# Two attention batches that sum keys and values in one pass each, with an instruction list arranged for it

## The chip, the cores and the metric

The kernel runs on one core of a Trainium2 chip. The metric is the device time of one execution in microseconds (us); lower is better. The core has a matrix engine (TensorE, in the profile PE, its weight loads PEld), VectorE (DVE), ScalarE (ACT), GpSimd (POOL) and SyncE (SP), each with its own queue of instructions that it works through in order. Engines wait for each other and for transfers through semaphores.

## The reference

Two stages. The first is an attention over 8 batches of 8 heads, 576 rows, 64 dimensions, in which keys and values are first pooled into 32 memory slots by a softmax of phi. The second is a bilinear feed-forward layer over all 4608 rows.

```python
a = exp(phi - max)                       # (8, 8, 576, 32)
a = a / (sum over the 32 slots)
k_m = einsum('bhsm,bhsd->bhmd', a, k)    # pooled keys, (8, 8, 32, 64)
v_m = einsum('bhsm,bhsd->bhmd', a, v)    # pooled values
scores = q @ k_m.T / sqrt(64)
attn = softmax(scores) @ v_m             # (8, 8, 576, 64)
x = attn, heads side by side             # (4608, 512)
out = ((x @ w_a) * (x @ w_b)) @ w_out    # w_a, w_b: (512, 1536), w_out: (1536, 512)
```

## The kernel before

Every instruction is issued from one list, the string `PLAN`, written out by hand or by a planner; the loop at the end of the kernel reads it token by token. So the order of tokens is the order of instructions on each engine. A wait in one instruction holds everything behind it on the same engine.

Tokens that begin with a digit are steps of that batch's attention:

- `exp0`, `exp1`: ScalarE takes the exponential of half of phi (L260).
- `qt0` to `qt3`: VectorE turns a quarter of q in 32 by 32 blocks (L269).
- `ks0`, `ks1` and `vs0`, `vs1` (`sums`): TensorE pools keys with a column of ones (L345, 128 columns), or values (64 columns), for one group of four heads, 36 matmuls each; VectorE then scales (L354, L355). `kt`, `vt` (`transpose`): small transposes into `kvT`, 8 for keys and 4 for values of a group (L363), and a copy (L366). These four serve batches 0 and 1 only.
- `kv` (`kv_sums`): keys, values and ones in one pass of 192 columns, 72 matmuls for all heads (L286). `km` (`take_kv`): VectorE scales into `rep` (L313, L318). `kvt` (`kv_transpose`): six full transposes and one copy (L326, L327). Batches 2 and later use `kv`.
- `s0`, `s1`: scores of a group (L380). `e0`, `e1`: ScalarE's exponential of them (L393). `den`: denominators by a matmul with `ones` (L403) and ScalarE's logarithm (L404). `nr`: ScalarE's exponential R (L412) and the product A on VectorE (L414). With a second digit, these take half of the rows.
- `hv`, `v` and `hx`, `x`: the fold of pooled values into 256 or 512 columns of w_a (a) or w_b (b) on TensorE (L449), and the copies of its result `vab` by ScalarE and VectorE (L462). The up projection then needs only A and `vab`.

The others: `aB.i.h` and `bB.i.h` are one half of an up projection of batch B, two matmuls (L624), then ScalarE's copy (L628) or VectorE's product into `ht` (L631). `dN` is N matmuls of the down projection (L553); `g`, `h`, `T` and `V` are its sums and differences on VectorE or POOL (L537, L520). `fN` and `FN` are N fill matmuls of 128 or 512 columns on a tile `warm`, whose results nobody reads (L211). `O` builds `ones` for the denominators, first on VectorE (L236), then on POOL (L237, L239). `M` is POOL's memset of the column of ones for batch 1's buffer (L642).

`pB`, `kB`, `vB`, `qB` load phi, k, v, q of a batch, `wLO:HI` a slice of columns of w_a and w_b, `oN` a part of w_out. All these are issued from POOL (L138 to L164). Phi keeps its four-byte type; k, v, q and weights become two-byte numbers on the way. `.0` or `.1` behind q is one half. Ahead of the list the kernel loads k of batch 0 in four-byte numbers on SP and ScalarE (L171; VectorE makes the cast, L217), then phi, q and v of batch 0 on POOL.

Of the kernel before, what the change touches and what calls it, by code (L numbers as in the profile page):

```python
# [35 lines left out]
a0.11.1 k2 d1 2exp0 g0.0 b1.6.1 b1.6.0 a1.9.1 h0.3 b0.11.1 v2 a0.10.1 b1.9.0 q2 T00 b0.10.1 T01 d1 a1.8.1 T21 d3
g0.1 V10 g0.2 d2 V20 a1.11.1 d1 2exp1 d1 V11 d3 b1.9.1 a1.10.0 a1.11.0 d3 b1.11.1 2kv 2km p3 b1.8.1 d1 q3 d4 k3
d2 a1.10.1 d9 a1.8.0 T31 d1 2kvt d1 2qt0 d2 2qt1 T30 3exp0 h1.0 d5 2qt2 d1 2qt3 d11 h1.1 b1.10.0 d1 3exp1
b1.11.0 d1 2sc g1.2 2e0 b1.8.0 g1.3 g2.0 v3 d1 2e1 d5 3qt0 d3 2den0 d1 2nr0 g2.1 d7 2v0 d1 3qt2 d1 p4 2den1 d5
2nr1 d7 p5 2x0b b1.10.1 2x0a d9 2v1 d3 a2.3.0 g2.2 a2.2.0 d2 3qt3 3qt1 2x1a d3 2x1b d1 a2.1.0 a2.0.0 h2.3 d3  # L40
# [1 line left out]
b2.0.0 p6 d1 b2.5.0 d7 b2.4.0 d1 3kvt a2.8.1 a2.7.0 d1 b2.8.0 d1 a2.6.0 b2.8.1 a2.11.1 d2 3sc 3e0 4qt0 d1 g3.1
d1 a2.7.1 d1 b2.7.0 d3 3e1 5exp0 d5 g3.2 b2.7.1 a2.11.0 4qt1 b2.6.0 b2.11.1 3den0 a2.4.1 d1 a2.5.1 b2.5.1 4qt2
d1 h3.3 d1 3nr0 a2.10.1 d1 b2.4.1 d3 b2.11.0 a2.0.1 d1 a2.9.0 d1 b2.10.1 4qt3 b2.9.0 d1 3den1 d1 a2.10.0 d1
b2.10.0 b2.0.1 d2 3v1 3x1a 4kv 3x1b 3v0b h4.0 3x0b a2.9.1 3nr1 d1 h4.1 h4.2 h4.3 a2.6.1 a2.3.1 a2.2.1 4km0 d1
4km1 4kvd b2.6.1 d2 5exp1 d13 b2.9.1 d2 3v2 3v0a 3x2b 3x2a d6 3x0a b2.2.1 d5 p7 a3.9.0 a3.11.0 b2.3.1 d3 5qt0
a3.1.0 b3.9.0 b3.1.0 b3.11.0 a3.3.0 d1 a3.0.0 b3.3.0 b3.0.0 v5 d4 a3.5.0 d4 a3.10.0 d2 b3.5.0 d2 4sc a2.1.1 d2
a3.10.1 d5 4e1 a3.4.1 d1 6exp0 b2.1.1 b3.10.0 4e0 4ed d1 b3.4.1 5qt3 g5.0 d3 a3.7.0 a3.8.1 b3.10.1 d1 a3.2.1
b3.8.1 b3.7.0 b3.2.1 a3.6.0 h5.1 d1 h5.3 b3.6.0 a3.1.1 q6 5qt1 a3.8.0 b3.1.1 h5.2 a3.3.1 a3.4.0 k6 a3.2.0 b3.2.0
b3.8.0 b3.3.1 d1 a3.6.1 4sm0 4v0a 5kv d1 5km0 d4 a3.9.1 d1 b3.4.0 4x0a d2 5km1 d1 h6.0 d4 a3.5.1 a3.7.1 v6 4tn0  # L50
d4 b3.6.1 b3.9.1 d2 h6.1 d4 a3.11.1 d1 4v1 4v0b d5 4x1b d1 a3.0.1 4x0b d1 4sm1 4x1a 5qt2 d1 6qt0 d1 b3.7.1 h6.2
4tn1 4ad 5kvd d9 4v2 d3 g6.3 d9 b3.11.1 d5 4x2a d10 b3.0.1 d1 6qt3 4x2b 7exp0 b3.5.1 6exp1 d3 h7.0 d9 a4.4.0
a4.0.0 a4.1.0 a4.5.0 b4.4.0 5sc 5e0 b4.0.0 a4.9.0 d1 5e1 b4.5.0 h7.1 b4.1.0 a4.11.0 b4.9.0 5v0 5x0a 6kv d1
a4.4.1 d1 h7.3 d1 6km0 d1 6km1 d1 5x0b 5ed d6 h7.2 d2 b4.4.1 a4.2.0 b4.11.0 a4.10.1 b4.10.1 b4.2.0 d1 h8.0
a4.6.1 d1 6kvd d1 5sm0 a4.1.1 a4.8.1 a4.7.0 5v1 6qt1 h8.1 q7 d1 5x1b b4.7.0 b4.6.1 k7 d2 b4.1.1 d3 5x1a d1
a4.2.1 a4.10.0 6qt2 b4.8.1 a4.6.0 5v2 5x2a 7exp1 d5 v7 b4.2.1 b4.6.0 d1 a4.8.0 d1 b4.10.0 a4.7.1 5x2b h8.3 d2
5tn0 d2 7qt0 b4.7.1 g8.2 d2 b4.8.0 a4.3.0 d7 5sm1 b4.3.0 d7 g9.0 d4 a4.9.1 d5 a4.3.1 d2 h9.1 d1 a4.5.1 d5 6sc d4
5tn1 6e1 d1 5ad b4.9.1 d1 a4.11.1 g9.2 d2 a4.0.1 d1 b4.5.1 b4.3.1 d3 6e0 d1 b4.0.1 g9.3 d1 b4.11.1 d4 6v0a 6v0b
6x0a 7kv d8 a5.2.0 7km0 d2 7km1 d2 7kvd d6 b5.2.0 6ed a5.2.1 6x0b b5.2.1 a5.11.0 d2 a5.9.0 a5.0.1 d4 b5.9.0 d8
7qt2 d1 h10.0 7qt1 d2 a5.3.1 g10.1 d8 b5.11.0 d1 b5.0.1 d2 h10.3 d1 a5.8.0 6sm0 a5.10.0 b5.3.1 b5.8.0 d4 a5.6.0  # L60
a5.1.1 b5.10.0 h10.2 7qt3 d1 a5.11.1 d3 a5.1.0 d1 b5.6.0 6tn0 d3 b5.1.1 a5.7.0 a5.0.0 b5.1.0 b5.11.1 a5.4.0
b5.0.0 b5.7.0 d2 a5.7.1 a5.4.1 b5.4.0 b5.7.1 d2 a5.3.0 6sm1 a5.10.1 6tn1 6v1 d1 6ad d1 6x1b b5.3.0 b5.4.1 d1
6x1a d1 b5.10.1 d3 6v2 d6 6x2b d1 6x2a a5.5.0 d1 b5.5.0 a5.9.1 a5.6.1 a5.5.1 7sc 7e1 7e0 a5.8.1 b5.6.1 b5.9.1
h11.0 b5.5.1 a6.0.0 b6.0.0 a6.3.0 d1 a6.10.0 b5.8.1 b6.3.0 a6.9.0 b6.10.0 d2 a6.7.0 h11.1 7v0a 7v1 h11.2 7x0a
a6.11.0 d5 g11.3 d4 b6.11.0 g12.0 d6 b6.7.0 7x1b d3 7ed d1 7sm0 d8 a6.3.1 d1 b6.9.0 d3 h12.1 d1 a6.2.1 d2 7sm1
7x1a d6 a6.9.1 g12.3 a6.5.0 d1 b6.3.1 d2 b6.2.1 g12.2 a6.8.1 b6.8.1 d1 a6.4.1 d3 b6.9.1 d1 a6.6.0 b6.5.0 a6.4.0
b6.6.0 d1 b6.4.1 d2 a6.8.0 a6.2.0 b6.4.0 b6.8.0 a6.1.0 7tn1 d2 a6.6.1 d3 b6.1.0 d3 b6.2.0 7tn0 a6.0.1 b6.0.1 d2
a6.5.1 d2 b6.6.1 7ad 7v0b 7v2 d1 7x2a d1 7x0b d1 a6.1.1 d3 g13.0 a6.11.1 d12 g13.1 b6.1.1 d2 7x2b h13.2 b6.5.1
d7 g13.3 b6.11.1 d2 a7.4.0 d1 a7.7.0 d3 a7.1.0 a7.6.0 d4 b7.1.0 b7.4.0 b7.6.0 d3 a6.10.1 b7.7.0 d2 a6.7.1 a7.0.0
d1 b6.7.1 b7.0.0 d8 a7.3.0 d3 b6.10.1 d1 h14.0 a7.2.0 a7.10.1 d1 a7.11.0 b7.3.0 d2 b7.11.0 a7.8.0 d1 b7.2.0  # L70
h14.1 b7.8.0 d1 a7.8.1 b7.8.1 b7.10.1 a7.4.1 d2 a7.5.0 b7.5.0 d2 b7.4.1 d2 a7.5.1 a7.9.1 d1 a7.3.1 g14.3 d2
a7.9.0 g14.2 d1 b7.5.1 b7.3.1 d6 b7.9.0 a7.10.0 b7.10.0 d7 b7.9.1 d4 a7.6.1 g15.0 d2 h15.1 d1 a7.1.1 a7.7.1 d5
h15.2 d1 g15.3 b7.1.1 d13 a7.2.1 d9 b7.6.1 d8 a7.0.1 d1 b7.2.1 d3 b7.0.1 b7.7.1 d1 a7.11.1 d2 b7.11.1 g16.0 d6
g16.1 d6 g16.2 d11 g16.3 d6 g17.0 h17.1 d40 h17.2 g17.3 d26
"""


# [611 lines left out]
```

## Time and profile before

| | |
|---|---|
| median of 3 runs | 236.83 us (236.38 to 236.87) |
| profiled execution, in all | 236.16 us |
| its span in the trace | 234.4 us |
| TensorE busy | 224.6 us, 96% of the span |
| VectorE busy | 185.0 us, 79% |
| ScalarE busy | 152.3 us, 65% |
| GpSimd busy | 120.0 us, 51% |
| read from and written to HBM | 42.47 MB, 9.44 MB |
| granted TensorE clock, mean | 0.996 of full speed |

The profile is of one execution. A line of its timeline gives the start in us, the length in us, engine, line and operation, what it writes and reads with their shapes, and how many instructions were merged (x8); in brackets stands how long the engine had stood idle and what ended that. A chain of waits is followed back from the last instruction to what released it, step by step. Spans on POOL are rough, and the ends of matmuls are modelled.

### The profile page before, as it was taken

The numbers are of one execution on the slowest core, as the hardware profiler recorded it, in microseconds if no ns is written. First come the engines' busy times: TensorE is split into PE (matmuls) and PEld (weight loads), VectorE is DVE, ScalarE is ACT, GpSimd is POOL, SyncE is SP. The second block draws the span as 40 slices with busy tenths as digits, with TensorE's granted clock in tenths as the row PEclk, the third lists the DMA queues.
The fourth block names the chain that finished last, engine by engine and source line by source line (L and its number), as shares of the span: only waits on it lengthen the run. The fifth ranks groups of instructions, "written<-read, shape, count | busy, mean of one in ns | idle before, by whom it ended". The sixth has DMA issues, their size and how long they took to land.

```text
span 234.4 us, 7699 instructions
## 1 busy us (share of the span) xinstructions
PE 224.6 (96%) x3059; PEld 169.9 (72%) x3059; DVE 185.0 (79%) x450; ACT 152.3 (65%) x398; POOL 120.0 (51%) x109
## 2 busy tenths in 40 slices
...
GB/s 230 239 252 203 207 207 206 229 235 257 213 224 289 202 240 196 130 229 118 190 183 169 111 137 227 164 110 77 26 166 3 92 50 92 45 48 51 41 137 134
DMA packets 38420, 37.27 MB, mean 159 GB/s; under 512 B 14672, under 2 KB 32464, under 8 KB 38384
## 3 DMA queue, kind: packets, MB, share of 16 engines
...
q10 hardware_dynamic: 512, 0.79, 1.0%
...
q14 instruction: 12, 0.10, 0.1%
HBM read 42.47 MB, written 9.44 MB: 221 GB/s over the span
## 4 chain that ended last, share of the span: by engine, by line
PE 77%; DMA 17%; POOL 3%; issue 1%; DVE 0%; POOLq 0%
PE py L553 19%; PE pa L624 18%; PE pb L624 18%; DMA kv_sb<-in_v_dram 12%; PE pv L553 10%; PE pva L449 5%; PE px L553 5%; DMA phi_sb<-in_phi_dram 5%; PE pkv L286 2%; POOL q_sb L150 1%; PE pscore L380 1%; POOL h_sums L537 1%; POOL phi_sb L138 0%; PE pk L345 0%; POOL kv_sb L145 0%
## 5 line engine op out<-in xcount | busy, mean ns | idle before, releaser
L631 DVE TENSOR_TENSOR ht<-a_sb,pb 128x288 f16<-128x288 f16 x192 | 79.9, 447 | 18.7 <-PE pb L624 9.0
L628 ACT CAST a_sb<-pa 128x288 f16<-128x288 f32 x192 | 71.5, 408 | 34.8 <-PE pa L624 28.9
L624 PEld LDWEIGHTS <-vab 128*128 128x128 f16 x768 | 73.5, 98 | 19.6 <-issue 4.5
L624 PE MATMUL pa<-A,vab 128*128 128x288 f16 x384 | 69.9, 286 | 0.9 <-DVE A L414 0.8
L624 PE MATMUL pb<-A,vab 128*128 128x288 f16 x384 | 70.5, 286 | 0.0
L553 PEld LDWEIGHTS <-h_sums 128*128 128x128 f16 x432 | 41.6, 98 | 10.4 <-issue 3.2
L537 POOL TENSOR_TENSOR h_sums<-ht 128x768 f16<-128x768 f16 x17 | 27.9, 1646 | 29.9 <-DVE ht L631 29.9
L553 PEld LDWEIGHTS <-ht 128*128 128x128 f16 x324 | 31.3, 98 | 6.3 <-issue 1.1
L553 PE MATMUL py<-w_sums,h_sums 128*128 128x256 f16 x216 | 35.2, 273 | 0.0
L462 ACT CAST vab<-pva 128x512 f16<-128x512 f32 (+1 forms) x60 | 31.6, 568 | 4.8 <-PE pva L449 4.1
L537 POOL TENSOR_TENSOR h_sums<-h_sums,ht 128x768 f16<-128x768 f16 x12 | 19.7, 1642 | 27.3 <-DVE h_sums L537 15.9
L462 DVE CAST vab<-pva 128x512 f16<-128x512 f32 (+1 forms) x44 | 26.8, 633 | 3.4 <-PE pva L449 3.1
L537 POOL TENSOR_TENSOR h_sums<-ht,h_sums 128x768 f16<-128x768 f16 x9 | 15.0, 1664 | 17.6 <-DVE h_sums L537 17.2
L260 ACT ACTIVATE exp_sb<-phi_sb 128x576 f16<-128x576 f32 x16 | 11.0, 698 | 12.4 <-DMA phi_sb<-in_phi_dram 12.4
L560 ACT ACTIVATE u<-py 128x256 f32<-128x256 f32 x36 | 14.1, 392 | 6.9 <-PE py L553 6.5
L553 PE MATMUL py<-wo_sb,ht 128*128 128x256 f16 x108 | 18.5, 273 | 0.0
L553 PE MATMUL pv<-wo_sb,h_sums 128*128 128x256 f16 x108 | 18.5, 273 | 0.0
L553 PE MATMUL px<-wo_sb,ht 128*128 128x256 f16 x108 | 18.4, 273 | 0.0
L553 PE MATMUL pv<-w_sums,h_sums 128*128 128x256 f16 x108 | 17.7, 273 | 0.0
L553 PE MATMUL py<-w_sums,ht 128*128 128x256 f16 x108 | 17.0, 272 | 0.0
L269 DVE STREAM_TRANSPOSE qT<-q_sb 128x288 f32<-128x288 f32 x32 | 14.0, 458 | 1.8 <-DMA q_sb<-in_q_dram 1.6
L211 PE MATMUL pw<-warm 128*128 128x128 f16 (+1 forms) x67 | 12.2, 334 | 1.3 <-DVE warm L180 1.3
...
## 6 DMA issues: line engine op xcount, KB each, us to landing
...
kv_sb<-in_v_dram POOLq DMA_DIRECT2D x8, 576.0 KB, 10.1
...
```

The source lines that it names most:

```text
L211: nc.tensor.matmul(pw[:, :cols], warm[:, :P], warm[:, :cols], start=True, stop=True)
L260: nc.scalar.activation(out=t["exp"][:, 2 * z:2 * z + 2, :, :], in_=phis[b][:, 2 * z:2 * z + 2, :].rearrange("p c (i m) -> p c i m", m=M), ...
L269: nc.vector.transpose(out=t["qT"][:, hp, :].bitcast(F32), in_=qs[b][:, hp, :].bitcast(F32))
L286: nc.tensor.matmul(t["pkv"][g][0][32 * j:32 * j + 32, 0:n], t["exp"][64 * r:64 * r + 64, hp, i, :], kvs[b][64 * r:64 * r + 64, 0:3 - given ...
L449: nc.tensor.matmul(t["pva", lo, z][g][0][32 * j:32 * j + 32, 0:hi - lo], t["kvT"][64 * r:64 * r + 64, 4 + g, M * j:M * j + M], w_sbs[z][64 ...
L462: engine_copy(out=vabs[b][z][:, g, lo:hi], in_=pva[:, 0:hi - lo])
L537: engine.tensor_tensor(out=out, in0=in0, in1=in1, op=op)
L553: nc.tensor.matmul(po, lhs[:, i], rhs[:, i], start=first and i == 0, stop=i == KH - 1, skip_group_check=not first)
L560: nc.scalar.mul(out=x, in_=po, mul=scale)
L624: nc.tensor.matmul(ps, vabs[b][x][:, g, P * i:P * (i + 1)], attn[b][:, g, HALF * hf:HALF * (hf + 1)], start=(g == 0), stop=(g == 1))
L628: nc.scalar.copy(out=a_sbs[b, i, hf], in_=ps)
L631: nc.vector.tensor_tensor(out=ht[:, i, t0:t0 + HALF], in0=a_sbs.pop((b, i, hf)), in1=ps, op=ALU.mult)
```

## The change

Batches 0 and 1 drop `ks`, `vs`, `kt` and `vt` and use `kv`, `km` and `kvt` as the later batches do. The joint pass needs v as well as k, so the load of v of batch 0 stands ahead of the two halves of q, and in the list v of batch 1 stands ahead of q of batch 1 and of the second slices of the weights. `M` moves from behind `v1` to ahead of `k1`, since the joint pass reads the column of ones with k and v. The first slices of the weights come ahead of phi of batch 1. The exponential of phi of batch 1 (`1exp0`) moves behind the exponentials of batch 0's scores. The whole list is arranged anew; only its beginning, and the place where q and v of batch 4 are loaded, are shown. It holds 53 fill matmuls of 512 columns for 37, and 81 of 128 columns for 30. No function changes, and every later batch keeps its steps; only the order in which they are interleaved is another.

```diff
-f3 F1 0qt0 f3 p1 F7 f4 f1 F6 F1 0exp0 f6 f1 f4 f6 f1 f1 0exp1 0ks0 0ks1 0qt3 w0:256 k1 O F7 0kt1 F2 1exp0 0kt0
-0qt2 0qt1 0s0 F5 0vs1 0vs0 w256:512 0vt1 q1.0 0s1 0e0 0vt0 0e1 F2 0hv0a 0hx0a 0den00 0nr00 q1.1 v1 0den10 0nr10
-M 1exp1 F3 0den01 a0.1.0 a0.0.0 0den11 0hv0b F3 0hx0b 1ks0 0nr01 0hv1a 1ks1 0hx1a 0nr11 b0.0.0 0hv1b 0hx1b 1kt1
-a0.2.0 1kt0 b0.1.0 a0.2.1 1qt0 1qt1 a0.0.1 1qt3 a0.1.1 1qt2 1s0 1e0 b0.1.1 1s1 1e1 b0.2.1 b0.2.0 1den0 b0.0.1
-1den1 1vs0 1vs1 1nr0 1vt0 1vt1 1nr1 a0.3.0 a0.3.1 1hv0a 1hv0b 1hv1a 1hx0a 1hx0b 1hx1a w512:1024 b0.3.0 b0.3.1
-a1.1.0 1hv1b 0v1a 0x1a a1.0.1 a1.0.0 1hx1b a1.3.0 b1.1.0 b1.0.0 w1024:1536 a1.1.1 b1.0.1 b1.3.0 b1.1.1 a1.3.1
-a0.5.0 b1.3.1 0v1b 1v1a 0x1b 1v1b o4 1x1a o3 a1.2.1 a0.7.0 1x1b b1.2.1 a1.2.0 b0.7.0 0v2a b0.5.0 0x2a a0.7.1
-a1.5.0 b1.2.0 a0.4.0 b0.7.1 a1.4.1 b1.5.0 b0.4.0 a0.4.1 a1.4.0 0v2b o1 1v2b 0x2b o0 1v2a 1x2a a0.9.1 b0.4.1
-b1.4.1 b0.9.1 a1.5.1 b1.4.0 o2 1x2b a0.8.1 b0.8.1 a0.11.0 b1.5.1 a0.6.0 a0.8.0 b0.11.0 b0.8.0 a0.6.1 a1.7.0
...
-b2.2.0 d3 q4 d1 b2.3.0 4exp0 2v2 2x2b 3kv 2x2a b2.1.0 d5 q5 d1 k4 a2.5.0 a2.4.0 v4 a2.8.0 3km 4exp1 k5 d1 h3.0
...
+f3 0qt0 f4 f2 f2 F3 F2 f1 0qt1 f6 F2 f1 w0:256 p1 F5 F8 f3 f1 f1 f2 F2 f2 0exp0 0exp1 F1 f6 F1 M f4 0kv F2 f3 F1
+k1 0km f1 F2 F4 0qt3 F3 O f1 0kvt F2 0s0 f2 0hv0b 0qt2 f1 0e0 0s1 0den00 f2 f4 0e1 f4 0hx0b f3 F1 0nr00 v1
+0den01 0hv0a F3 1exp0 0nr01 F5 0den10 0den11 F5 f2 f1 0hx0a 0nr10 1exp1 a0.1.0 q1.0 b0.1.0 a0.0.0 b0.0.0
+w256:512 f2 1kv 0nr11 F1 a0.1.1 1km a0.0.1 f1 f4 b0.1.1 0hv1a 0hx1a 1kvt a0.2.0 a0.3.0 q1.1 a0.2.1 0hv1b 1hv0b
+1qt0 1hv0a 1qt1 1hx0b 1hx0a 1s0 1hv1b f1 f2 f2 f1 1e0 1qt3 1qt2 1hx1b w512:1024 0hx1b 1den0 1s1 1hv1a 1e1 b0.2.0
+b0.0.1 1nr0 b0.3.0 w1024:1536 1den1 f2 f4 b0.2.1 1nr1 0v1a 1hx1a a0.3.1 b0.3.1 a1.1.1 a1.1.0 o0 0x1a a1.0.1
+b1.1.1 b1.1.0 b1.0.1 a1.0.0 b1.0.0 a1.3.1 a1.3.0 b1.3.1 b1.3.0 a0.5.0 p2 0v1b 0x1b 1v1b 1v1a o1 0v2a 1x1a 0x2a
+a1.2.0 a0.7.0 b0.5.0 a1.2.1 b1.2.0 b1.2.1 1x1b a1.5.0 a0.7.1 b0.7.0 b0.7.1 a0.4.0 a0.4.1 b1.5.0 b0.4.0 a0.9.1
...
+2e1 d10 2den0 d1 h2.2 d1 p5 2v0 2x0b 3qt0 g2.3 d2 2den1 d2 2nr0 d4 2nr1 3qt1 d15 2x0a d1 q4 2v1 2x1a d1 3qt2 d8
+3qt3 2x1b d1 g3.0 d1 a2.4.0 a2.3.0 d2 h3.1 d2 a2.1.0 b2.1.0 2v2 3kv k5 h3.2 2x2a d1 2x2b a2.5.0 b2.4.0 4exp0
+h3.3 b2.3.0 a2.8.0 a2.2.0 k4 b2.5.0 b2.2.0 v4 a2.0.0 5exp0 b2.8.0 d1 a2.11.0 q5 d2 4exp1 d1 a2.7.0 d1 p6 a2.8.1
...
     nc.scalar.preload_act_table_set("natural_log_exp_and_others")
     load_phi(0)
     kvs[0] = kv_sbs[0]
+    load_v(0)
     for x in halves:
         load_q(0, x)
-    load_v(0)
 
     warm = consts.tile([P, 512], F16, name="warm")
     nc.vector.memset(warm, 0.0)
```

More of the change, by code (lines that the diff above doesn't have):

```diff
@@ L31 @@
-a1.1.0 1hv1b 0v1a 0x1a a1.0.1 a1.0.0 1hx1b a1.3.0 b1.1.0 b1.0.0 w1024:1536 a1.1.1 b1.0.1 b1.3.0 b1.1.1 a1.3.1
-a0.5.0 b1.3.1 0v1b 1v1a 0x1b 1v1b o4 1x1a o3 a1.2.1 a0.7.0 1x1b b1.2.1 a1.2.0 b0.7.0 0v2a b0.5.0 0x2a a0.7.1
-a1.5.0 b1.2.0 a0.4.0 b0.7.1 a1.4.1 b1.5.0 b0.4.0 a0.4.1 a1.4.0 0v2b o1 1v2b 0x2b o0 1v2a 1x2a a0.9.1 b0.4.1
-b1.4.1 b0.9.1 a1.5.1 b1.4.0 o2 1x2b a0.8.1 b0.8.1 a0.11.0 b1.5.1 a0.6.0 a0.8.0 b0.11.0 b0.8.0 a0.6.1 a1.7.0
-b0.6.0 a0.5.1 a1.7.1 b0.6.1 a0.9.0 b0.5.1 b1.7.0 a0.10.0 b1.7.1 b0.9.0 b0.10.0 o5 a1.6.1 p2 a1.6.0 a1.9.0
@@ L36 @@
[L36 to L40, printed above, removed]
@@ L41 @@
-b2.2.0 d3 q4 d1 b2.3.0 4exp0 2v2 2x2b 3kv 2x2a b2.1.0 d5 q5 d1 k4 a2.5.0 a2.4.0 v4 a2.8.0 3km 4exp1 k5 d1 h3.0
[L42 to L74, printed above, removed]
+f3 0qt0 f4 f2 f2 F3 F2 f1 0qt1 f6 F2 f1 w0:256 p1 F5 F8 f3 f1 f1 f2 F2 f2 0exp0 0exp1 F1 f6 F1 M f4 0kv F2 f3 F1
@@ new lines @@
+b1.1.1 b1.1.0 b1.0.1 a1.0.0 b1.0.0 a1.3.1 a1.3.0 b1.3.1 b1.3.0 a0.5.0 p2 0v1b 0x1b 1v1b 1v1a o1 0v2a 1x1a 0x2a
+a1.2.0 a0.7.0 b0.5.0 a1.2.1 b1.2.0 b1.2.1 1x1b a1.5.0 a0.7.1 b0.7.0 b0.7.1 a0.4.0 a0.4.1 b1.5.0 b0.4.0 a0.9.1
+b0.4.1 0v2b 1v2a 0x2b 1x2a 1v2b a1.4.0 a1.4.1 a0.11.0 o2 b0.9.1 o5 a0.8.0 b1.4.0 b1.4.1 a0.6.1 o4 b0.11.0 b0.8.0
+a1.5.1 1x2b a0.8.1 b0.6.1 k2 2exp0 a1.7.0 a0.6.0 b1.5.1 b0.8.1 b0.6.0 a0.9.0 b1.7.0 b0.9.0 a1.7.1 o3 a0.5.1
+b1.7.1 a0.10.0 a0.10.1 b0.10.0 a1.9.0 b0.5.1 a0.11.1 d1 a1.6.1 g0.0 h0.3 b0.10.1 b0.11.1 a1.6.0 b1.6.1 T00
@@ new lines @@
+b1.9.0 a1.8.1 v2 q2 b1.6.0 T01 d1 a1.9.1 T21 d1 p3 2exp1 g0.1 V20 k3 V10 g0.2 q3 V11 a1.11.0 b1.9.1 d5 b1.11.0
+d2 a1.8.0 2kv p4 d1 b1.8.1 d2 2km d4 a1.10.1 d1 3exp0 d1 T31 a1.10.0 d11 2qt0 d1 T30 2qt1 b1.10.0 d1 2kvt
+a1.11.1 d1 2qt2 d1 3exp1 h1.0 d2 b1.8.0 2qt3 d2 h1.1 d13 g1.2 d3 b1.11.1 g1.3 b1.10.1 2sc g2.0 g2.1 2e0 d4 v3 d2
+2e1 d10 2den0 d1 h2.2 d1 p5 2v0 2x0b 3qt0 g2.3 d2 2den1 d2 2nr0 d4 2nr1 3qt1 d15 2x0a d1 q4 2v1 2x1a d1 3qt2 d8
+3qt3 2x1b d1 g3.0 d1 a2.4.0 a2.3.0 d2 h3.1 d2 a2.1.0 b2.1.0 2v2 3kv k5 h3.2 2x2a d1 2x2b a2.5.0 b2.4.0 4exp0
@@ new lines @@
+h3.3 b2.3.0 a2.8.0 a2.2.0 k4 b2.5.0 b2.2.0 v4 a2.0.0 5exp0 b2.8.0 d1 a2.11.0 q5 d2 4exp1 d1 a2.7.0 d1 p6 a2.8.1
+d1 3km b2.0.0 b2.11.0 d3 a2.7.1 d4 4qt0 d1 3kvt d10 b2.8.1 d2 5exp1 d1 b2.7.1 d1 3sc d1 3e1 3e0 b2.7.0 a2.4.1 d2
+b2.4.1 a2.9.0 a2.10.0 d1 b2.9.0 a2.0.1 a2.5.1 3den0 4qt3 d2 b2.10.0 b2.5.1 d2 a2.6.0 d1 b2.0.1 a2.11.1 d1 4qt1
+b2.6.0 a2.10.1 3den1 d1 b2.10.1 d3 b2.11.1 d1 h4.0 3v1 3x1a 4kv 3v0b 3x1b h4.1 a2.2.1 4km0 d1 3x0b a2.6.1 d1
+3nr0 d3 4km1 d1 4kvd d1 a2.3.1 a2.9.1 d4 3nr1 b2.2.1 d3 b2.6.1 d2 b2.9.1 h4.3 d2 3v2 3v0a 3x2a d1 3x0a d5 a3.5.0
@@ new lines @@
+h4.2 3x2b v5 d2 a3.11.0 b2.3.1 4qt2 d1 a3.3.0 d2 5qt0 a3.1.0 d1 b3.5.0 a3.9.0 b3.1.0 b3.11.0 d1 b3.9.0 d6 p7
+b3.3.0 4sc d2 4e1 a3.0.0 d3 a2.1.1 a3.10.0 d3 a3.8.1 d2 b3.0.0 d6 5qt3 b2.1.1 a3.10.1 b3.10.0 a3.2.1 4e0 d1 4ed
+a3.4.1 h5.0 d1 h5.1 b3.10.1 b3.8.1 h5.3 d1 q6 b3.2.1 d2 a3.7.0 h5.2 5qt2 d1 a3.1.1 5qt1 6exp0 b3.7.0 a3.6.0
+b3.4.1 a3.8.0 d1 b3.6.0 b3.1.1 k6 a3.3.1 b3.8.0 d2 a3.4.0 d1 a3.6.1 b3.4.0 b3.3.1 d4 4sm0 d3 a3.2.0 4v0a 5kv
+4x0a 5km0 d1 5km1 b3.6.1 a3.7.1 d3 a3.9.1 a3.11.1 d9 b3.2.0 d1 4v0b 4x0b 4v1 d1 4x1a d5 g6.0 4tn0 v6 6qt0 h6.1
@@ new lines @@
+h6.2 b3.7.1 d3 b3.9.1 4x1b b3.11.1 a3.5.1 4sm1 4tn1 4ad d1 5kvd d1 6exp1 d5 g6.3 d7 4v2 d7 a3.0.1 d1 b3.5.1 6qt1
+d13 b3.0.1 d2 4x2b d9 4x2a d4 g7.0 d1 a4.1.0 a4.0.0 g7.1 a4.4.0 a4.5.0 5sc 5e1 b4.1.0 b4.0.0 5e0 b4.5.0 a4.10.1
+d1 b4.4.0 5v0 6kv d2 5x0b h7.2 d1 a4.9.0 d1 6km0 6km1 d6 b4.10.1 d1 h7.3 d2 a4.1.1 d5 5x0a d2 b4.9.0 d1 a4.7.1
+7exp0 a4.4.1 a4.6.1 b4.1.1 b4.7.1 a4.3.0 h8.0 b4.4.1 b4.6.1 h8.1 5ed a4.2.1 b4.3.0 6kvd d1 h8.3 k7 d1 a4.10.0
+a4.2.0 5v1 5x1a 5sm0 b4.2.0 d1 a4.6.0 v7 b4.2.1 b4.6.0 q7 5x1b d1 5sm1 7exp1 d3 a4.11.0 d15 g8.2 b4.10.0 d1 6qt2
```

18 lines of the change are left out of this document (added).

## The prediction

> **What bounds it now.** I read the busy table by stages first, to see where TensorE has room. Columns: stretch, its length, then for each engine busy us (instructions), granted TensorE clock, DMA share, GB/s.
>
> ```profile
> 15.00:20.00 5.00, 4.11 (x115) 1.96 (x114) 1.75 (x6) 3.67 (x11) 3.47 (x4) 1.00 1.31 204
> 20.00:25.00 5.00, 4.13 (x115) 2.21 (x114) 2.55 (x10) 3.43 (x10) 2.70 (x4) 1.00 1.33 202
> 25.00:30.00 5.00, 4.38 (x67) 2.24 (x68) 4.50 (x13) 3.65 (x12) 1.62 (x3) 1.00 1.22 207
> 30.00:35.00 5.00, 4.82 (x141) 3.13 (x142) 4.35 (x14) 4.76 (x14) 1.41 (x2) 1.00 1.24 206
> 35.00:40.00 5.00, 5.00 (x63) 3.08 (x62) 4.69 (x12) 4.49 (x13) 1.47 (x2) 1.00 1.25 209
> ```
>
> From about 30 us TensorE has no gap; from 40 us to the end its waits come to 0.3 us. Before 30 us it is padded with fill matmuls (the two L211 forms: 10.6 and 2.7 us of busy time) and the transfers run at their limit. The chain of waits says the same (start, length, what):
>
> ```profile
> 4.99 11.25 DMA phi_sb<-in_phi_dram
> 16.53 13.38 DMA kv_sb<-in_v_dram
> 29.96 0.83 PE pk L345 x72
> 31.39 0.60 PE pa L624 x4
> ```
>
> So there are two regimes: data-bound to 29.96 us, then TensorE work without a break to 230.6 us. In the second, any useful TensorE work left over costs its full length; in the first it costs nothing. The question is what each list still has to do once TensorE is full. The rows that time the start:
>
> ```profile
> 9.12 0.48 DVE L269 STREAM_TRANSPOSE qT<-q_sb 128x288 f32<-128x288 f32 x1 [1.65 <-DMA q_sb<-in_q_dram]
> 16.27 0.68 ACT L260 ACTIVATE exp_sb<-phi_sb 128x576 f16<-128x576 f32 x1 [7.16 <-DMA phi_sb<-in_phi_dram]
> 16.86 1.29 ACT L393 ACTIVATE E<-pscore 128x288 f16<-128x288 f32 x4
> 21.82 0.75 POOL L159 DMA_DIRECT2D wa_sb<-in_moe_w_a_dram  x1 [1.10 <-DMA kv_sb<-in_k_dram]
> 22.96 0.30 PE L449 MATMUL pva<-wa_sb,kvT 64*32 64x256 f16 x8 [0.34 <-DMA wa_sb<-in_moe_w_a_dram]
> 24.28 0.30 PE L449 MATMUL pva<-wb_sb,kvT 64*32 64x256 f16 x8 [0.16 <-DMA wb_sb<-in_moe_w_b_dram]
> ```
>
> They date landings: first half of q of batch 0 at 9.1, phi of batch 1 at 16.25, k of batch 1 at 21.8, the second weight slices at 22.9 and 24.25, v of batch 1 at 29.93. The joint run already exists for batch 2:
>
> ```profile
> 55.50 0.94 PE L286 MATMUL pkv<-kv_sb,exp_sb 64*32 64x192 f16 x72
> 56.48 0.17 DVE L313 RECIPROCAL rphi<-pkv 128x1 f32<-128x1 f32 x1 [0.22 <-PE pkv L286]
> 56.68 0.74 DVE L318 TENSOR_SCALAR rep<-pkv,rphi 128x256 f16<-128x256 f32 x2
> 58.97 0.50 PE L326 MATMUL pT<-ident,rep 128*128 128x128 f16 x6
> 59.51 0.56 DVE L327 COPY kvT<-pT 128x768 f16<-128x768 f16 x1 [0.21 <-PE pT L326]
> ```
>
> **TensorE work removed.** Batch 0 has 1.26 (k sums) + 0.77 (v sums) + 0.59 + 0.48 (turns) = 3.1 us; batch 1 has 0.68 + 0.68 + 0.60 + 0.77 + 0.57 = 3.3 us. Each becomes 0.94 + 0.50 = 1.44, so some 3.5 us go. But in the old list only v of batch 1 stands in the full regime: from 29.96 to 31.39, 1.43 us. That is all that the edit as such can bring; the rest goes out of time that was padded anyway.
>
> **Landings after.** From phi of batch 0 (7.85) to phi of batch 1 (16.25) 1728 KB land, 206 KB/us; from k to v of batch 1, 1664 KB in 8.1 us, 205. The queue lands in the order of issue, so 576 KB cost 2.8 us, 288 KB 1.4, 256 KB 1.25. New order: v0 10.6, halves of q0 12.05 and 13.45, first weight slices 14.7 and 15.95, phi1 18.8, k1 21.8 (the same bytes stand ahead of it), v1 24.6, first half of q1 26.0, second weight slices 27.3 and 28.5, second half of q1 29.95. From there all is as before. Against the old list v1 gains 5.3 us and the second weight slices lose 4.3.
>
> A rule speaks for faster landings: the Trainium skill, "DMA: Bandwidth & Descriptors", section "Bandwidth", measures 425 GB/s for a large load on one core. v1 and all ahead of it read 8.1 MB (k, v, q and weights are read in four-byte numbers), so with that page's 2 us of fixed cost it would land near 21 us (an estimate from the page), below the row's 24.6. The row decides, being this queue with these casts; the rule's case is a rival below.
>
> **POOL's queue.** The 2.04 us memset of the ones column moves ahead of k1, which is then issued near 10.5, with transfers queued until 18.8: hidden. The build of `ones` (O) stands ahead of v1 and waits on VectorE's memset, near 15.4; so v1 is issued near 16.1 (old order: 16.53), 5 us before its data's turn at 21.8: hidden too. Were it not, v1 would slip one for one. From the ninth load on, each waits for the one eight before it, which here has always landed.
>
> **Start of batch 0.** v0 at 10.6 releases the joint sums, 10.65 to 11.6; the fills ahead end just before. VectorE has the first two q turns ahead of its work on the sums: q at 12.05, turns to 13.0 (0.48 and 0.42), then two times 0.17 + 0.74 to 14.8. Six transposes to 15.4, copy to 16.0 (0.56), scores 16.05 to 16.5 (0.45), exponentials from 16.55. The old list has them at 16.86, because ScalarE stood behind the exponential of phi1 (7.16 us idle before 16.27); that one goes behind them now. So the late start of batch 0 is made good here: 0.3 us early.
>
> Next ScalarE works through its new order at its spacing in rows of several (0.30 us for 288 columns: four in 1.29 above, one alone takes 0.41; 0.58 for an exponential of 576, two in 1.26): 16.55 to about 21.6 for the third R. VectorE makes A by 21.95, and the first up projections run from 22.0 to 23.0 (old: from 20.4, since it took both groups' first halves first).
>
> **Start of batch 1.** On TensorE its joint sums stand next, and wait from 23.0 to 24.6, with all behind them: the other up projections of the first slice. Sums to 25.5, VectorE 1.8 to 27.3; up projections (0.245 us a half) to 26.75; the fold over the second slice at 27.35, its landing. Turn to 28.0, copy to 28.6, two q turns to 29.45, scores to 29.95, exponentials to 30.7, the denominator matmul 31.0, then scores of group 1 to 31.4, exponentials 32.45, second denominators 32.75. ScalarE: R of group 0, L twice, R of group 1 at 34.4; VectorE A 0.46 to 34.85. So the first up projection of batch 1 (a1.1.1) starts near 34.9; ahead of it TensorE has stood about 0.6 (fold), 0.3 (denominators) and 0.8 us (A), with fills besides. After it come twelve such halves and folds whose weights are there.
>
> **Sum.** At 34.9 the new list has done, beyond what the old one has at 29.96: v sums and turns of batch 1 (1.43 us), its four 256-column folds (0.49), one 512-column fold (0.28), two a and two b halves (0.98): 3.18 us. The old list has done them at 33.14. So the new one is 34.9 − 33.1 = **1.8 us late**, and TensorE cannot win it back. On the profiled execution (span 234.4, 236.16 in all) that is 237.9; on the median 236.83, 0.7 above it, 238.6.
>
> The rest of the list is costed at nothing: it has the same 384 up halves and 756 down steps, 95 of them after the last up projection in both, and TensorE at work throughout is the cover. A changed order can be worth ±0.5 us; in the old one a wait of 0.3 us on v of batch 4 shows (near 89 us). In the new order three POOL additions of 1.65 us stand between the issues of q and v of batch 4, where none does now; transfers are queued there, which hides it; if not, v slips by up to 5 us and TensorE with it.
>
> **Rivals.** (1) Faster: transfers land early enough that neither the joint sums nor the fold wait, and the chain through ScalarE keeps up; then the 1.43 us of batch 1 show, less some 0.3 of waits: 235.7. It decides from the point where a1.1.1 starts before 33.1. For it: 3.5 us of TensorE work really go, and ScalarE no longer waits for phi1. Against: the second slices land 4.3 us later by plain order of bytes. (2) The page's rate: v1 before 23.0, sums start right after the up projections, 1.6 us early, and what follows with them, if weights and q come as early: 237.0, within a few tenths of no change. Against: the rows at 205 KB/us over 22 us. (3) ScalarE and VectorE, 4.35 to 4.76 of 5 us busy from 30 to 40 now, get the folds of batch 1 bunched with its softmax and hold TensorE beyond a1.1.1: another 1.5 to 2, 240.3. (4) The edit doing nothing is excluded by the list: 144 sums matmuls and 36 small transposes go.
>
> **Numbers.** My case (0.6 to 2.9 us slower, 237.4 to 239.7) 0.66; rival 3 0.10; rival 2 0.12; rival 1 0.12. About 0.2% is what a measurement of this kernel can tell from no change: 0.5 us. Rival 2 gives most of "same", with a few hundredths to each side: faster 0.13, same 0.10, slower 0.77. The range takes in my case, half of rival 2 and most of rival 3: 236.9 to 240.2.
>
> **What would show it.** In the changed profile: first joint sums (L286) near 10.7, released by v; exponentials of the scores (L393) near 16.6; the second L286 run near 24.6 with v as releaser; first L449 on the second slice near 27.3, released by the weights; first up projection of batch 1 near 34.9 behind A (L414); more fill time (L211 has 53 matmuls of 512 columns for 37, 81 of 128 for 30); no gap from 36 us on. I am wrong if v1 lands by 23, or if a1.1.1 comes before 33.

## The result, and the profile after

The changed kernel takes 238.23 us (median of 14 runs, 237.49 to 240.23). Beside it the kernel before ran at 236.85 us (14 runs, 235.47 to 238.21). The ratio is 1.0064, with a 95% interval of 1.0039 to 1.009: the change makes the kernel slower, by 1.4 us between the medians. The profiled execution took 237.83 us with a span of 236.1, against 236.16 and 234.4. So 1.7 us are to be found in the traces. (Here and below, medians and ranges take in every run, ratios only those within 1.5% of the fastest of their kernel.)

First the busy table by stages for the changed kernel, with the columns of the one shown for the kernel before:

```profile
15.00:20.00 5.00, 4.53 (x80) 2.40 (x79) 1.37 (x3) 2.35 (x8) 4.93 (x9) 1.00 1.18 266
20.00:25.00 5.00, 4.74 (x78) 2.82 (x82) 2.04 (x6) 4.21 (x11) 1.89 (x4) 1.00 1.25 205
25.00:30.00 5.00, 4.62 (x124) 2.69 (x105) 4.74 (x16) 2.72 (x9) 2.54 (x4) 1.00 1.31 203
30.00:35.00 5.00, 4.62 (x72) 2.92 (x65) 4.14 (x12) 4.80 (x14) 1.40 (x2) 1.00 1.24 207
35.00:40.00 5.00, 4.95 (x66) 3.47 (x64) 4.99 (x12) 4.58 (x12) 1.45 (x2) 1.00 1.24 228
```

TensorE is busier from 15 to 25 us than it was (4.53 and 4.74 of 5 us for 4.11 and 4.13), with fewer matmuls (80 and 78 for 115 and 115). This is padding, not progress: the fills now come to 24.2 us of busy time (15.4 of 512 columns and 8.8 of 128), against 13.3. From 20 to 35 us the transfers still move 203 to 207 GB/s. The start is as data-bound as it was.

The rows of the timeline that time the start, from several engines (start, length, what; the idle time before it in brackets):

```profile
11.44 0.94 PE L286 MATMUL pkv<-kv_sb,exp_sb 64*32 64x192 f16 x72
16.82 0.71 ACT L393 ACTIVATE E<-pscore 128x288 f16<-128x288 f32 x2 [7.81 <-PE pscore L380]
24.49 0.94 PE L286 MATMUL pkv<-kv_sb,exp_sb 64*32 64x192 f16 x72
27.09 0.30 PE L449 MATMUL pva<-wa_sb,kvT 64*32 64x256 f16 x8 [0.33 <-DMA wa_sb<-in_moe_w_a_dram]
34.60 0.78 PE L624 MATMUL pa<-A,vab 128*128 128x288 f16 x5
```

The joint sums of the two batches stand at 11.44 and 24.49 (L286). The fold over the second slice of the weights waits for its data at 27.09; before, it ran at 22.96. The first up projection of batch 1 starts at 34.60.

How late that is can be read from a count. At 50 us both lists have done the same work for batches 0 and 1 but for the up projections. These are TensorE's groups from 0 to 50 us (busy us and mean ns of one behind the first bar), before:

```profile
L624 PE MATMUL pa<-A,vab 128*128 128x288 f16 x76 | 13.4, 287 | 0.8 <-DVE A L414 0.8
L624 PE MATMUL pb<-A,vab 128*128 128x288 f16 x72 | 12.8, 287 | 0.0
```

and after:

```profile
L624 PE MATMUL pa<-A,vab 128*128 128x288 f16 x72 | 12.6, 286 | 0.4 <-DVE A L414 0.3
L624 PE MATMUL pb<-A,vab 128*128 128x288 f16 x68 | 11.9, 286 | 0.0
```

That is 148 against 140 matmuls. A pair of them takes 0.245 us, so the 8 that are missing are 0.98 us.

The rest shows at the joint sums of batch 4, the only place behind 36 us where TensorE stands still for long. Before:

```profile
89.14 0.94 PE L286 MATMUL pkv<-kv_sb,exp_sb 64*32 64x192 f16 x72 [0.32 <-DMA kv_sb<-in_v_dram]
```

and after, with the step ahead of it:

```profile
89.38 0.40 PE L449 MATMUL pva<-wb_sb,kvT 64*32 64x512 f16 x8
90.72 0.94 PE L286 MATMUL pkv<-kv_sb,exp_sb 64*32 64x192 f16 x72 [0.94 <-ACT vab L462]
```

Ahead of it both lists have run the same 268 up matmuls and 155 of the down projection, so the two times can be compared: the same instruction is 1.58 us late, and its wait has grown from 0.32 to 0.94. The bracket names ScalarE's copy of `vab`, which ends at 90.70, but `kv` waits for several things at once, and the copy is only the last that the profile shows. POOL's queue shows what else was late. Before:

```profile
73.70 0.78 POOL L145 DMA_DIRECT2D kv_sb<-in_v_dram  x1
```

and after:

```profile
71.47 0.79 POOL L150 DMA_DIRECT2D q_sb<-in_q_dram  x1
73.14 1.64 POOL L537 TENSOR_TENSOR h_sums<-h_sums,ht 128x768 f16<-128x768 f16 x1 [0.89 <-PE pa L624]
74.99 0.78 POOL L142 DMA_DIRECT2D kv_sb<-in_k_dram  x1 [0.21 <-issue]
75.79 1.65 POOL L537 TENSOR_TENSOR h_sums<-ht,h_sums 128x768 f16<-128x768 f16 x1
77.39 1.65 POOL L537 TENSOR_TENSOR h_sums<-ht 128x768 f16<-128x768 f16 x1
78.98 0.78 POOL L142 DMA_DIRECT2D kv_sb<-in_k_dram  x1
79.75 0.75 POOL L145 DMA_DIRECT2D kv_sb<-in_v_dram  x1
```

The load of v of batch 4 (L145) is issued at 79.75 instead of 73.70. Three additions of 1.65 us and k of batch 5 have come between it and q of batch 4. It lands 10.8 us later, at 90.58; before, it landed at 89.01. So the sums start 0.13 to 0.14 us behind this landing in both kernels, but in the changed one the copy ends just as late, and only an experiment can tell the two apart.

### The profile page after: what moved, and what is told of

It reads as the page before. It is cut to its first block, busy times and chain, and to the rows that moved or that the text cites. A ratio compares the mean times of both kernels' runs of the same rounds, so it can differ in the third digit from the quotient of the medians.

```text
span 236.1 us, 7480 instructions
## 1 busy us (share of the span) xinstructions
PE 228.4 (97%) x2946; PEld 173.7 (74%) x2946; DVE 187.4 (79%) x439; ACT 152.2 (64%) x398; POOL 127.8 (54%) x114
## 4 chain that ended last, share of the span: by engine, by line
PE 85%; DMA 8%; DVE 2%; POOL 1%; ACT 1%; issue 1%; DVEq 0%; POOLq 0%
PE py L553 21%; PE pa L624 20%; PE pb L624 20%; PE pv L553 10%; PE pva L449 5%; PE px L553 5%; DMA wa_sb<-in_moe_w_a_dram 4%; DMA q_sb<-in_q_dram 4%; PE pkv L286 2%; PE pscore L380 1%; ACT vab L462 1%; DVE rep L318 1%; PE pD L403 1%; DVE qT L269 1%; DVE ht L631 1%
## 5 line engine op out<-in xcount | busy, mean ns | idle before, releaser
L628 ACT CAST a_sb<-pa 128x288 f16<-128x288 f32 x192 | 72.8, 409 | 35.6 <-PE pa L624 27.5
L624 PE MATMUL pa<-A,vab 128*128 128x288 f16 x384 | 71.5, 286 | 0.4 <-DVE A L414 0.3
L537 POOL TENSOR_TENSOR h_sums<-ht 128x768 f16<-128x768 f16 x20 | 32.6, 1638 | 42.0 <-DVE ht L631 42.0
L553 PEld LDWEIGHTS <-h_sums 128*128 128x128 f16 x432 | 41.6, 98 | 10.8 <-issue 3.2
L553 PE MATMUL py<-w_sums,h_sums 128*128 128x256 f16 x216 | 38.9, 273 | 0.0
L537 POOL TENSOR_TENSOR h_sums<-ht,h_sums 128x768 f16<-128x768 f16 x13 | 21.3, 1640 | 15.7 <-DVE h_sums L537 6.0
L537 POOL TENSOR_TENSOR h_sums<-h_sums,ht 128x768 f16<-128x768 f16 x10 | 16.4, 1638 | 13.4 <-DVE h_sums L537 12.1
L211 PE MATMUL pw<-warm 128*128 128x128 f16 (+1 forms) x134 | 21.1, 312 | 1.3 <-DVE warm L180 1.3
L393 ACT ACTIVATE E<-pscore 128x288 f16<-128x288 f32 x32 | 11.3, 422 | 10.8 <-PE pscore L380 10.8
L211 PEld LDWEIGHTS <-warm 128*128 128x128 f16 x134 | 11.4, 109 | 9.2 <-issue 2.7
L553 PE MATMUL pv<-wo_sb,h_sums 128*128 128x256 f16 x108 | 17.7, 272 | 0.0
```

The lines of the kernel that those rows point to most:

```text
L211: nc.tensor.matmul(pw[:, :cols], warm[:, :P], warm[:, :cols], start=True, stop=True)
L393: nc.scalar.activation(out=Ev[:, g, :, z, :], in_=pss, func=AF.Exp, scale=1.0 / (8.0 * CS))
L537: engine.tensor_tensor(out=out, in0=in0, in1=in1, op=op)
L553: nc.tensor.matmul(po, lhs[:, i], rhs[:, i], start=first and i == 0, stop=i == KH - 1, skip_group_check=not first)
L624: nc.tensor.matmul(ps, vabs[b][x][:, g, P * i:P * (i + 1)], attn[b][:, g, HALF * hf:HALF * (hf + 1)], start=(g == 0), stop=(g == 1))
L628: nc.scalar.copy(out=a_sbs[b, i, hf], in_=ps)
```

## The experiments

Two explanations were held against their rivals. The first: the start costs about 1 us, because v of batch 1 and the second slices of the weights (the joint sums, the fold) arrive later than the work that needs them did in the old list; its rival puts the loss into the start of batch 0. The second: the load of v of batch 4 costs the rest; its rivals are that the bracket is right and ScalarE holds the sums, or that the time would be lost elsewhere anyway. All ratios are to the kernel before, run on the same chip; its medians in the three sets of runs were 237.09, 237.21 and 237.31 us. Of the lists only the stretches that change are shown.

### The load of v of batch 4, early, in the changed kernel

```diff
-d15 2x0a d1 q4 2v1 2x1a d1 3qt2 d8
+d15 2x0a d1 q4 k4 v4 2v1 2x1a d1 3qt2 d8
...
-a2.8.0 a2.2.0 k4 b2.5.0 b2.2.0 v4 a2.0.0
+a2.8.0 a2.2.0 b2.5.0 b2.2.0 a2.0.0
```

> The changed kernel with the loads of k and v of batch 4 issued right behind q of batch 4, ahead of two POOL additions and of k of batch 5. Theory C (the 0.94 us wait ahead of the joint sums of batch 4 is for v of batch 4, issued 6 us later than before): the wait goes, the time falls by 0.6 to 0.9 us to 237.5. Theory D (the wait is for ScalarE's copy of the fold, which frees a bank, as the profile's bracket names it): no change, 238.2, and the wait stays near 0.9 us.

Measured 236.62 us (22 runs, 236.34 to 237.07), ratio 0.9985 (0.9974 to 0.9997). This is the timeline of TensorE there:

```profile
89.32 0.40 PE L449 MATMUL pva<-wb_sb,kvT 64*32 64x512 f16 x8
89.53 0.95 PE L286 MATMUL pkv<-kv_sb,exp_sb 64*32 64x192 f16 x72
```

Only the place of two loads was changed, and the sums follow the fold without a bracket. So the wait was for the load, not for ScalarE's copy. Its removal takes 1.19 us out of the profile (90.72 to 89.53) and 1.6 us out of the median, more than was expected, and the runs spread over 0.7 us where they spread over 2.7: this wait differs from run to run.

### The same in the kernel before

```diff
-b2.2.0 d3 q4 d1 b2.3.0 4exp0
+b2.2.0 d3 q4 k4 v4 d1 b2.3.0 4exp0
...
-q5 d1 k4 a2.5.0 a2.4.0 v4 a2.8.0
+q5 d1 a2.5.0 a2.4.0 a2.8.0
```

> The kernel before with k and v of batch 4 issued right behind q of batch 4, ahead of q of batch 5. Theory C (both kernels wait for v of batch 4 near 90 us, and its landing sets most of the difference): its own wait, 0.3 us in the profile and more in slow landings, goes, and the runs draw together, 236.1 to 236.5. Then the changed kernel with the same repair (236.6) is 0.2 to 0.5 slower by its start alone. If the start costs nothing: 236.6, the same as that one.

Measured 235.73 us (13 runs, 235.28 to 236.67), ratio 0.9949 (0.9927 to 0.9971), below the range that was expected. The sums start without a wait:

```profile
88.64 0.95 PE L286 MATMUL pkv<-kv_sb,exp_sb 64*32 64x192 f16 x72
```

The kernel before paid for this load too, 0.50 us in the profile (89.14 to 88.64).

The two kernels with the load early differ in the start of the list and its arrangement, not in this wait. They stand 0.89 us apart in the medians (236.62 less 235.73), 0.89 at the sums of batch 4 (89.53 less 88.64), and 7 up matmuls at 50 us (141 for 148, 0.86 us). That is the price of the start. The 1.58 us by which the sums of batch 4 were late divide into 0.89 of start and 0.69 of a longer wait (1.19 less 0.50). Those are single executions on two chips; the ratios, in which each kernel is held against the kernel before on its own chip, say the same: the start is 0.0036 (0.9985 less 0.9949), or 0.85 us, the load costs the changed kernel 1.9 us and the kernel before 1.2, and the 0.7 between them and the start make up the 1.5 us of the result's 1.0064.

### The load issued late in the kernel before

```diff
-q5 d1 k4 a2.5.0 a2.4.0 v4 a2.8.0 3km 4exp1 k5 d1 h3.0
+q5 d1 a2.5.0 a2.4.0 a2.8.0 3km 4exp1 k5 d1 h3.0 k4 v4
```

> The kernel before with k and v of batch 4 issued later: behind q and k of batch 5 and one POOL addition, some 4 us later. Theory C: TensorE waits at the joint sums of batch 4 for 2 us or more and the time rises to 238 to 240, without any change in batches 0 and 1. Rival (there is enough cover, the change's loss is its start): within 0.4 of before.

Measured 241.43 us (6 runs, 239.96 to 244.02), ratio 1.0171 (1.0133 to 1.0209). The load goes out at 78.28 instead of 73.70. First the sums in TensorE's timeline, then the stages around them (the column ahead of the last two is the granted clock):

```profile
93.03 1.29 PE L286 MATMUL pkv<-kv_sb,exp_sb 64*32 64x192 f16 x72 [3.86 <-DMA kv_sb<-in_v_dram]
```

```profile
94.00:96.00 2.00, 2.00 (x30) 0.99 (x15) 1.10 (x3) 1.20 (x3) 0.00 (x0) 0.50 0.04 8
96.00:98.00 2.00, 2.00 (x16) 1.53 (x14) 1.93 (x9) 1.92 (x5) 1.57 (x2) 0.78 0.00 0
```

Here the load is named. Issued 4.6 us later, the sums start 3.9 us later, nearly one for one. The clock is at half for 3.4 us behind the wait (93.46 to 96.88), which is why the time rises beyond the 238 to 240 expected: against the kernel with the early load the sums of batch 4 are 4.4 us late, those of batch 5, with the same work between them, 6.0 us (115.38 for 109.39).

### Batch 0 apart again

The changed kernel with the early load, but batch 0 as it was: q ahead of v, sums and turns by group, fills cut to suit.

```diff
-f3 0qt0 f4 f2 f2 F3 F2 f1 0qt1 f6 F2 f1 w0:256 p1 F5 F8 f3 f1 f1 f2 F2 f2 0exp0 0exp1 F1 f6 F1 M f4 0kv F2 f3 F1
-k1 0km f1 F2 F4 0qt3 F3 O f1 0kvt F2 0s0 f2 0hv0b 0qt2 f1 0e0 0s1 0den00 f2 f4 0e1 f4 0hx0b f3 F1 0nr00 v1
+f3 0qt0 f4 f2 f2 F3 F2 f1 0qt1 f6 F2 f1 w0:256 p1 F5 f3 f1 f1 0exp0 0exp1 0ks0 0ks1 F4 f6
+k1 0kt0 0qt3 F3 0kt1 O F2 0s0 0qt2 0e0 f4 0s1 0den00 F3 0vs0 0vs1 0vt0 0vt1 0hv0b 0e1 f4 0hx0b f3 F1 0nr00 v1 M
...
-    load_v(0)
     for x in halves:
         load_q(0, x)
+    load_v(0)
```

> The changed kernel with v of batch 4 early and with batch 0 taken back to apart sums, q ahead of v, its scores near 13 and its v sums behind them. Theory A: the joint sums of batch 1 still start at 24.4 and everything after is as in the changed kernel with v of batch 4 early: 236.6 (within 0.3), although batch 0 starts 3 us sooner. Theory B: 236 or less.

Measured 236.66 us (22 runs, 236.43 to 237.22), ratio 0.9981 (0.9967 to 0.9994): the same as with batch 0 joint (236.62). Its timeline tells why:

```profile
21.75 0.29 PE L624 MATMUL pa<-A,vab 128*128 128x288 f16 x1
...
24.24 0.94 PE L286 MATMUL pkv<-kv_sb,exp_sb 64*32 64x192 f16 x72 [0.82 <-PE pw L211]
...
26.95 0.30 PE L449 MATMUL pva<-wa_sb,kvT 64*32 64x256 f16 x8 [0.44 <-DMA wa_sb<-in_moe_w_a_dram]
```

The first up projection is 1.1 us earlier than with both batches joint (22.83), but the joint sums of batch 1 only 0.19 us earlier (24.43 there), after a wait of 0.82, and the fold 0.08 (27.03). The bracket names a fill, which ended just before the wait. The exponential of phi, the other thing that the sums need late, ended at 22.46; v, issued at 13.56, took 10.6 us to land, 24.15, and is what they waited for. In this list batch 0 has slack; what arrives for batch 1 sets the pace.

A first form of this experiment had the load of v of batch 4 late and the value sums of batch 0 ahead of the second group's scores:

> The changed kernel with batch 0 taken back: q of batch 0 is loaded ahead of v again, batch 0 sums and turns k and v apart, and the ones column of batch 1 is filled behind v1. Theory A (the loss arises in batch 1: its joint sums hold TensorE until v1 lands at 24.5, the fold on the second weight slices until 27.1, and the first up projection of batch 1 comes at 34.6): the first scores of batch 0 come 2 us or more earlier, and the time stays at the changed kernel's, 238.2 (within 0.4), with the joint sums of batch 1 still at 24.5. Theory B (the late start of batch 0 costs: first up projection 22.9 for 20.4): it goes back to 237 or below.

Measured 239.09 us (9 runs, 237.38 to 243.2), ratio 1.0079 (1.0045 to 1.0114). Neither theory holds, and it can't be read as the price of batch 0: TensorE waited 1.58 us for v of batch 0 where the list had no cover, the clock fell to half, and the sums of batch 4 waited 1.32 us besides.

### Batch 0 joint, alone, in the kernel before

```diff
+    load_v(0)
     for x in halves:
         load_q(0, x)
-    load_v(0)
...
-0exp1 0ks0 0ks1 0qt3 w0:256 k1 O F7 0kt1 F2 1exp0 0kt0
-0qt2 0qt1 0s0 F5 0vs1 0vs0 w256:512 0vt1 q1.0 0s1 0e0 0vt0
+0exp1 0kv 0km 0qt3 w0:256 k1 O F7 0kvt F2 1exp0
+0qt2 0qt1 0s0 F5 w256:512 q1.0 0s1 0e0
```

> The kernel before with batch 0 alone made joint (v of batch 0 ahead of q), batch 1 and the order of all other loads as before. Theory A: exponentials of the scores still wait for phi of batch 1, near 16.9, all that follows is as before, so 236.8 as before (within 0.4). Theory B: batch 0's later start costs 1 us or more, 237.8.

Measured 238.73 us (21 runs, 236.94 to 240.74), ratio 1.0059 (1.0038 to 1.0079), with waits of 2.19 us for v of batch 0 ahead of its joint sums and of 1.85 us at the sums of batch 4. So it was run with the early load as well:

> The kernel before with batch 0 alone made joint, and v of batch 4 early. Theory C: the 238.7 of the run with batch 0 joint was mostly its wait of 1.85 us for v of batch 4; with that gone 236.3 to 236.9, the rest being a wait of 0.6 us for a bank near 33.9. Theory B (late start of batch 0 costs): 237.5 or more.

Measured 237.17 us (22 runs, 236.0 to 237.79), ratio 0.9994 (0.9977 to 1.0011), 1.4 us above the kernel before with the early load. The result lies between the two theories. A loss is clear, and the traces date part of it: the joint sums wait 1.60 us for v of batch 0, the first up projection comes 1.04 us later (20.63 for 19.59), and the value sums of batch 1 start 0.48 us later (30.41 for 29.93), no longer held by v. So in this list the slack of batch 0 was used up. The rest lies behind that, where TensorE waits 0.5 us for a bank of PSUM; its cause is not shown. The list was not arranged for a joint batch 0 (fills of 1.25 us stand between the two groups' scores). In the changed list the price is nothing, by the experiment above.

### The order of loads alone

The kernel before with the early load; v of batch 1 and the first half of its q stand ahead of the second slices of the weights, as in the changed kernel, and the sums stay apart.

```diff
-0s0 F5 0vs1 0vs0 w256:512 0vt1 q1.0 0s1
+0s0 F5 0vs1 0vs0 v1 0vt1 q1.0 w256:512 0s1
...
-0nr00 q1.1 v1 0den10
+0nr00 q1.1 0den10
```

> The kernel before with v of batch 4 early and one thing of the change: v and the first half of q of batch 1 are loaded ahead of the second weight slices. Sums stay apart and the list stays as it was. Theory A (the change's start loses because the second slices land 4 us later): the fold over the second slice waits from 22.9 to 27.1 with all of TensorE's queue behind it, and the wait for v of batch 1 near 29.8 goes; without a list arranged for it the time rises by 2 to 4 us over 235.7, against 0.9 in the changed kernel. If the order of these loads costs nothing: 235.7 to 236.2.

Measured 241.28 us (6 runs, 240.39 to 241.82), ratio 1.0141 (1.01 to 1.0182). TensorE's timeline, and one stage:

```profile
27.19 0.42 PE L449 MATMUL pva<-wa_sb,kvT 64*32 64x256 f16 x8 [4.56 <-DMA wa_sb<-in_moe_w_a_dram]
27.38 1.19 PE L345 MATMUL pk<-kv_sb,exp_sb 64*32 64x128 f16 x36
```

```profile
27.00:29.00 2.00, 1.81 (x46) 1.20 (x46) 0.36 (x2) 0.71 (x2) 0.93 (x2) 0.50 1.24 206
```

The second slices arrive at the time that they have in the changed kernel (27.19 against 27.09), so this is the order's doing and not that of the joint sums. In the old order of work it costs a wait of 4.56 us and a halved clock: the sums after it take 1.19 us, where the same sums ahead of it took 0.68. At 50 us 104 up matmuls are done for 148, 5.4 us, where 2 to 4 were expected. Read beside the changed kernel, the new arrangement hides most of a loss which the new order of loads makes, and leaves 0.9; how much of the 0.9 is the wait for v and how much the second slices was not run apart.

### Two without a clear effect

The column of ones written behind v of batch 1 in the changed kernel, as in the kernel before:

```diff
-F1 f6 F1 M f4 0kv F2 f3 F1
+F1 f6 F1 f4 0kv F2 f3 F1
...
-0hx0b f3 F1 0nr00 v1
+0hx0b f3 F1 0nr00 v1 M
```

> The changed kernel with POOL's memset of the ones column moved back behind v1. Theory A: VectorE's casts of k of batch 0 take 1.6 us again in place of 4.7, which ran beside that memset, but the joint sums of batch 0 still start at 11.4 behind the fills, and the time stays at 238.2 (within 0.3). If the casts were what held the start: 0.5 to 1 us less.

Measured 238.79 us (6 runs, 238.08 to 241.55), ratio 1.0107 (1.0057 to 1.0157), which holds the changed kernel's 1.0064. The casts on VectorE are shorter (below), but the sums of batch 0 start at 11.30 for 11.44. The profiled execution waits 2.04 us for v of batch 4, although its load was issued as before (79.71 for 79.75): v landed at 91.64 for 90.58, so this landing varies by a microsecond with nothing changed ahead of it.

And phi of batch 1 behind the softmax of batch 0, in the kernel before with the early load:

```diff
-f3 F1 0qt0 f3 p1 F7 f4
+f3 F1 0qt0 f3 F7 f4
...
-0qt3 w0:256 k1 O F7 0kt1 F2 1exp0 0kt0
-0qt2 0qt1 0s0 F5 0vs1 0vs0 w256:512 0vt1 q1.0 0s1 0e0 0vt0 0e1 F2
+0qt3 w0:256 p1 k1 O F7 0kt1 F2 0kt0
+0qt1 0s0 0e0 0qt2 0s1 F4 0vs1 0vs0 w256:512 0vt1 q1.0 0e1 0vt0 F2
...
-M 1exp1 F3 0den01 a0.1.0 a0.0.0 0den11 0hv0b F3 0hx0b 1ks0 0nr01
+M F3 0den01 a0.1.0 a0.0.0 0den11 0hv0b F3 0hx0b 0nr01 1exp0 1exp1 1ks0
```

> The kernel before with v of batch 4 early and with one idea of the changed list: the first weight slices are loaded ahead of phi of batch 1, and the exponentials of phi of batch 1 stand behind batch 0's softmax, so that ScalarE does not stand 7 us for it. Theory A: first up projections some 2 us earlier, but data-bound to v of batch 1 at 29.9 as before, so little of it shows: 235.2 to 235.8. Rival (ScalarE's 7 us were a real cost): 234.5 or less. A worse list: 236 or more.

Measured 235.66 us (10 runs, 235.28 to 236.79), ratio 0.9928 (0.99 to 0.9955): no difference from the kernel without it (235.73, 0.9949) that the intervals can tell. The first up projections come 0.8 us earlier (18.77 for 19.59), and the key sums of batch 1 then wait 0.92 us for that exponential. At the sums of batch 4 0.29 us are left (88.35 for 88.64). Again an earlier batch 0 gives little.

## Why the prediction was right

**The direction and the sum.** It said 238.6, within 236.9 to 240.2; 238.23 was measured. For the profiled execution it worked out 237.9, and that was 237.83. But this closeness is partly luck: the start was taken for too much, and a cost that was set at nothing makes up for it.

**The start of batch 0.** Exponentials of the scores were expected at 16.55 and came at 16.82. Inside, the steps were less exact: the joint sums start at 11.44, not 10.65, because the fills ahead of them ran at half rate until 7.05 us and so ended late. That cost nothing, since VectorE takes its first two turns of q ahead of its work on the sums, and q landed at 11.83 (12.05). That the start of batch 0 has slack is shown by the kernel with batch 0 apart.

**The start of batch 1.** The list of landings held, within 0.4 us but for one (w_b's first slice, 17.21 for 15.95): the joint sums at 24.49 (24.6), the fold on the second slice at 27.09 (27.35), the first up projection of batch 1 at 34.60 (34.9). One thing in it was off: TensorE does not wait for v from 23.0 to 24.6. The first up projections themselves come at 22.89 instead of 22.0, so that v (24.34) is there when they are done. Nor had the load eight places ahead always landed: POOL waits for it 0.94 us at 21.71 and 2.17 us at 24.63, but no wait of TensorE for these later weights shows. With the up projections earlier the wait for v appears (0.82 us, in the kernel with batch 0 apart).

**The size of the start was the mis-sized term**: 1.8 us, measured 0.9 to 1.0. About 0.3 of the difference is the new list, which reached its point sooner (34.60 for 34.9). Another 0.3 lies on the other side: the old list was taken to do 3.18 us of work right behind 29.96, at 33.14, without a gap. By count it has that work, and two up matmuls (0.245 us) more, at 33.70, so it reached the point at about 33.46; its stage shows 4.82 of 5 us busy from 30 to 35. That leaves the new list some 1.1 us late there, and 0.98 by the count at 50 us. The last 0.2 us were not followed.

**The rest of the list, costed at nothing, is the step that did not hold.** The prediction saw the three additions ahead of the load of v of batch 4 and judged that queued transfers hide it. They hid some 4.5 us of the 6 (issue at 79.75 for 73.70, sums at 90.72 for 89.14), the later start covered 0.9, and 0.7 us of added wait came through: the fallback named there, in small. The wait of 0.3 us in the old trace was the hint: with a wait there already, no slack was left that could cover anything.

**The rivals.** Faster: fell, since a1.1.1 came at 34.60, not before 33.1; the 1.43 us that the edit removes beyond 30 us are real but smaller than what the order of loads takes. The rate of the Trainium skill ("DMA: Bandwidth & Descriptors", section "Bandwidth", 425 GB/s), with v by 23: fell, since v landed at 24.34. But the rate itself agrees with the trace. The rows' 203 to 207 GB/s count bytes as written; k and v of batch 1 are read at twice that size (2.36 MB), landed between 18.77 and 24.34, and so come to 424 GB/s as read. The estimate was 3 us early for other reasons: half of that is there at the first landing, phi of batch 0, at 7.74, where the page's rate and fixed cost give 6.2 (an estimate, from 1.77 MB of k and phi); the other half is spread over the loads between. ScalarE and VectorE holding TensorE: VectorE is busy 4.99 of 5 us from 35 to 40, but TensorE 4.95, so that it lost 0.05 us there.

**A better kernel.** The kernel before with k and v of batch 4 issued right behind its q is the best here: 235.73 us, ratio 0.9949, and with phi of batch 1 moved 235.66, no different within the noise. Both beat both kernels of this change.
